# Earlier loads and new step places in the last pair of a fused attention and mixture-of-experts kernel

## The chip, the cores and the metric

One core of a Trainium2 chip. The time is the device time of one execution in microseconds (us), the median of three runs. A profile comes from one more execution, whose own time is given too.

## What is computed

```python
scores = scale * np.matmul(q, k.transpose(0, 1, 3, 2))          # B, H, S, D = 4, 8, 576, 64
scores = scores + bias.transpose(2, 0, 1)[None, :, :, :]        # a small MLP of relative positions
attn = np.exp(scores - np.max(scores, axis=-1, keepdims=True))
attn = attn / (np.sum(attn, axis=-1, keepdims=True) + 1e-09)
x = np.matmul(attn, v).transpose(0, 2, 1, 3).reshape(B * S, H * D)   # 2304 tokens of 512
logits = x @ w_gate
e_idx = np.argmax(logits, axis=1)                                # one of 8 experts for each token
for e in range(E):
    h = np.maximum(x[mask] @ w1[e], 0.0)                         # 512 to 1024
    out[mask] = gate_w[mask, None] * eom[mask, e, None] * (h @ w2[e])
```

## The kernel before, in words

**Attention.** Heads are worked on two at a time: 4 batches of 4 pairs make 16 pairs. The steps of a pair are written as words in strings, and a loop over n = 0 to 16 (L895) emits the words of one string for each n. `ORDER` serves most pairs, `LAST` is the string of n = 15 and `END` that of n = 16. A word names a step and a copying engine; each `-` at its end means one pair earlier than n, each `+` one later. `s` words score a block of 128 queries: matmuls (L763, L778), then a VectorE instruction that adds the bias and finds the maximum (L743), then the exponential on ScalarE (L748). `t` words transpose the exponentials on TensorE (L799, L811) and copy them from PSUM to `et` on ScalarE or VectorE (L803, L814). `a` words multiply with v (L831) and copy the result to `xt` (L832). PSUM has three buffers for transposes and logits (`pt`), and one for `a` (`pa`).

**v.** A pair's v lies in `vt`. The second head also needs `vb`, a copy shifted by 64 rows (loaded at L695 and L696 by the word `b`), and `vz`, a zero-padded block that GpSimd copies from `vb` (L697). There is one `vb` buffer, so the last pair's `vb` is loaded after the word `a2a-` of the pair before it.

**Work steps.** The list `work` holds generators: logits (L502), routing of a batch (L193), routing of a group of tokens (`route_group`, L245). The words `w` and `u` advance the first of them by one step. The first expert slot's loads and splits are such steps too: `first_w2` (L463) goes to the front of the list when the third score block is done, `first_w1` (L440), `first_x` (L445) and eight `first_split` (L450) go to its end.

**Experts.** The tokens are sorted into slots of 288 tokens of one expert. A slot gathers its tokens with three indirect DMAs of GpSimd (`gather`, L426), transposes them (`x`, L436 to L438), and multiplies with w1 and w2 (L1000, L1021). fp32 is split in a high and a low part. Slot 0's w1 is split in eight halves, the high part by a cast of ScalarE (L456), the low part by a subtraction on GpSimd:

```python
        nc.scalar.copy(out=w1h[c][:, h], in_=w1r[c][:, h])
        nc.gpsimd.tensor_tensor(
            out=w1l[c][:, h], in0=w1r[c][:, h], in1=w1h[c][:, h].bitcast(F32), op=ALU.subtract
        )
```

After the eighth, slot 1's w1 is loaded to the same buffers. Each later slot splits its weights with ScalarE and VectorE (L419, L420). All weights and v are loaded through the queue of SyncE (SP), which issues in program order and stops at the first load whose buffer is still in use.

**Logits.** For each third of the queries: four matmuls of `xt` (L507), a copy to `ls` on ScalarE (L530), and in the next step transposes (L537, L549) and a product with `rec` on VectorE (L540), summed into logits (L545). In the first third's first step VectorE makes `rec` from `sums`:

```python
            V.tensor_scalar(out=rec, in0=sums_t[b], scalar1=1e-9, scalar2=None, op0=ALU.add)
            V.reciprocal(out=rec, in_=rec)
```

Of the kernel before, what the change touches and what calls it, by code (L numbers as in the profile page):

```python
# [9 lines left out]
F32 = mybir.dt.float32  # L10
# [10 lines left out]
B, H, S, D = 4, 8, 576, 64  # L21
HID = 32
NPAIR = H // 2
DM, DFF, NE = 512, 1024, 8
# [4 lines left out]
G = 96  # L29
# [23 lines left out]
)  # L53

LAST = (
    "s2 s1 w u a0d- t10a- s3 u w t11a- s0 u t12a- s6 t20d- u s7 b- t04d u t01d t03a s8 u t02a a1a- "
    "s5 t00d w s4 u a2a- a0d w t14d t13a u t21d u t12a u t20d "
)

END = (  # L60
    "t10a- t11d- x a1d- x w a2a- x w x w w w w "
)


# [68 lines left out]
def attention_moe_kernel(  # L133
# [15 lines left out]
    nc = tc.nc  # L149
# [4 lines left out]
    biasp = ctx.enter_context(tc.tile_pool(name="biasp", bufs=1))  # L154
# [4 lines left out]
    vp = ctx.enter_context(tc.tile_pool(name="vp", bufs=2))  # L159
# [243 lines left out]
    w1r, w1h, w1l, w2r, xs, xg = [], [], [], [], {}, {}  # L403
# [36 lines left out]
    def first_w1():  # L440
        for i, (p, t) in enumerate(((qx, "qt0"), (qx, "qs0"), (spl, "h"), (spl, "l"))):
            w1r.append(p.tile([128, DFF], F32, name=f"w1r{i}", tag=t))
        load_w1(0)

    def first_x():  # L445
        t = nat.tile([G, 2, DM], F32, name="xg0", tag="nat")
        xg[0] = [t[:, 0, :], t[:, 1, :], vp.tile([G, DM], F32, name="xg0_2", tag="v")]
        gather(0)

    def first_split(i):  # L450
        if i == 0:
            for m, to in enumerate((w1h, w1l)):
                t = biasp.tile([128, 4, DFF], F32R, name=f"w1_{m}", tag=f"bias{m}")
                to.extend(t[:, c, :] for c in range(4))
        c, h = i // 2, slice(i % 2 * 512, i % 2 * 512 + 512)
# [4 lines that stand above are left out]
        if i == 7:  # L460
            load_w1(1)
# [11 lines left out]
    work = []  # L473
# [4 lines left out]
    def do_work(any_of=None):  # L478
        for todo in any_of or (rows, work):
            if todo:  # L480
                try:
                    next(todo[0])
                except StopIteration:
                    todo.pop(0)
                break
# [103 lines left out]
    with ExitStack() as actx:  # L589
        pool = lambda name, bufs, **kw: actx.enter_context(tc.tile_pool(name=name, bufs=bufs, **kw))  # L590
        kq = pool("kq", 2)
# [9 lines left out]
        o, n = _WHERE["psi"]  # L601
        early = hb.tile([128, 144 + 36], F32, name="early", bufs=1)
        bc, cinv = early[:, 0:144], early[:, 144:180]
        ot, n = _WHERE["tab"]
# [67 lines left out]
        kl_t, v_t, vb_t, nat_t = {}, {}, {}, {}  # L672
# [17 lines left out]

        def emit_load_vb(b, pr):

            vb = vp.tile([128, 5, D], F32, name="vb", tag="vb", bufs=1)
            src = v[b, 2 * pr + 1]
            nc.sync.dma_start(out=vb[:, 0:4, :], in_=src[0:512].rearrange("(n p) d -> p n d", p=128))  # L695
            nc.sync.dma_start(out=vb[0:64, 4, :], in_=src[512:S])  # L696
            nc.gpsimd.tensor_copy(out=vz[2][0:64], in_=vb[0:64, 4, :])  # L697
            vb_t[b, pr] = vb

        vz = []  # L700

# [132 lines left out]
        pairs = [(b, pr) for b in range(B) for pr in range(NPAIR)]  # L834
        begun = " ".join(BEGIN.values()).split()
# [31 lines left out]
        for hl in range(2):  # L867
            for i, w in enumerate((wg, wog)):
                nc.sync.dma_start(
                    out=wgb[hl * 64:hl * 64 + 64, :, hl * 16 + i * 8:hl * 16 + i * 8 + 8],  # L870
                    in_=w.rearrange("(a t d) e -> t d a e", t=2, d=64)[hl],
# [10 lines left out]
        def first(f, *a):  # L882
            yield from ()
            f(*a)

        chunks = [0, 1, 2, 3]

        def copies(c):
            return nc.scalar.copy if c == "a" else V.tensor_copy
# [5 lines left out]
        for n in range(len(pairs) + 1):  # L895
            if n == 2:
                work.extend(first(emit_zero, r0) for r0 in range((B - 1) * S, NTOK, 96))
            if n == len(pairs) - 1:
                work.append(first(first_w1))
            todo = {i: 1 for i in range(8)}  # L900
            for op in orders.get(n, ORDER).split():
                name = op.rstrip("+-")
                m = n + op.count("+") - op.count("-")
                if name == "w":
                    do_work()
                elif name == "u" and n >= len(pairs) - NPAIR:
                    do_work((work,))
                elif name == "x":
                    transpose_x(0, chunks.pop(0))
                if name in "wux" or not 0 <= m < len(pairs) or m == 0 and name in begun or m == 1 and name[0] == "p":  # L910
                    continue
                b, pr = pairs[m]
                i = int((name + "0")[1])
                if name == "s8":
                    emit_s4(b, pr)
                elif name[0] == "s":
                    emit_s(b, pr, i // 2, i % 2)
                    if m == len(pairs) - 1:

                        todo.pop(i)  # L920
                        if i < 4 and not any(j in todo for j in range(4)):
                            work.append(first(first_x))
                            work.extend(first(first_split, j) for j in range(8))
                        if i > 5 and not any(j in todo for j in (6, 7)):
                            work.insert(0, first(first_w2))
                        if i in (4, 5) and not any(j in todo for j in (4, 5)):
                            t = biasp.tile([128, 4, 4, CH], F32R, name="x", tag="bias2")
                            xs.update({j: (t[:, 2 * j], t[:, 2 * j + 1]) for j in range(2)})
                elif name[0] == "t":
                    emit_t(  # L930
                        b, pr, i, int(name[2]), copies("a" if name[0:3] in to_act and b == B - 1 else name[3])
                    )
                elif name[0] == "a":
                    emit_av(b, pr, i, copies(name[2]))
                    if i == 2 and m == len(pairs) - 2:
                        emit_load_vb(*pairs[-1])
                    if pr == NPAIR - 1:
                        work.append(emit_logits(b, i))
                        if i == 2:
                            work.append(emit_route(b))  # L940
                            if b >= B - 2:
                                work.append(route_group(b - (B - 2)))
                elif name[0] in "kp":
                    (emit_kq, emit_place)["kp".index(name[0])](b, pr, i)
                else:
                    {"l": emit_load, "v": emit_load_v, "b": emit_load_vb, "z": emit_q4}[name](b, pr)
        t = biasp.tile([G, 3, DM], F32, name="xg1", tag="bias4")
        xg[1] = [t[:, j, :] for j in range(3)]
        gather(1)
        while chunks:  # L950
            transpose_x(0, chunks.pop(0))
# [197 lines left out]
```

## Time and profile before

| | us |
|---|---|
| median of 3 runs (lowest to highest) | 645.22 (643.30 to 646.17) |
| profiled execution, its own time | 646.73 |
| its span | 644.9 |
| PE (TensorE matmul) busy | 592.7 (92%) |
| DVE (VectorE) busy | 432.6 (67%) |
| ACT (ScalarE) busy | 385.0 (60%) |
| POOL (GpSimd) busy | 83.8 (13%) |

PEld is TensorE's weight load, SP is SyncE; a name with q (SPq) is an engine's queue. The first 87 us make the bias, up to some 390 us the pairs run, then the expert slots. The page cuts the span in 40 slices of 16.1 us; the 24th, from 371 to 387 us, is the only one between the sixth and the last in which PE is busy for less than 80%.

### The profile page before, as it was taken

How to read it: one execution, taken by the hardware profiler on the slowest of the kernel's cores; microseconds unless marked ns; L12 is line 12 of the kernel's file. 1: busy time of each engine (PE TensorE's matmuls, PEld its weight loads, DVE VectorE, ACT ScalarE, POOL GpSimd, SP SyncE). 2: the span in 40 equal slices, each digit the busy share in tenths (PEclk: the TensorE clock that was granted, in tenths of full speed). 3: DMA queues.
4: the chain of work that ended last, by engine and by line, in shares of the span. 5: the costliest groups of instructions: out<-in, count | busy, mean ns of one | idle time of the engine just before them, and what ended most of it. 6: DMA issues, size and time to landing. Idle time of an engine off the chain costs nothing.

```text
span 644.9 us, 13582 instructions
## 1 busy us (share of the span) xinstructions
PE 592.7 (92%) x5036; PEld 498.2 (77%) x5036; DVE 432.6 (67%) x1011; ACT 385.0 (60%) x784; POOL 83.8 (13%) x140
## 2 busy tenths in 40 slices
PE   5887779999999999999898879999999999999992
PEld 2333368887888778887776648999999999999971
DVE  5958657766787667875898547677876465555560
ACT  5687657777776767777655644445544454454550
POOL 1000000000000000000000145021321304041010
PEclk9978979999999999999999989999999999999997
DMA  6997784765666656564643457566656555565410
GB/s 142 212 204 172 196 174 102 179 150 115 132 139 170 154 121 133 134 167 103 139 130 75 167 182 228 173 205 228 206 163 238 170 196 189 181 208 167 132 38 8
DMA packets 99846, 101.90 MB, mean 158 GB/s; under 512 B 71395, under 2 KB 71651, under 8 KB 99764
## 3 DMA queue, kind: packets, MB, share of 16 engines
q1 hardware_dynamic: 93616, 86.11, 51.9%
q0 software_dynamic: 3392, 10.03, 5.0%
q10 hardware_dynamic: 2756, 4.72, 2.1%
q8 instruction: 45, 0.74, 0.5%
q14 instruction: 37, 0.30, 0.1%
HBM read 60.73 MB, written 10.81 MB: 111 GB/s over the span
## 4 chain that ended last, share of the span: by engine, by line
PE 70%; issue 11%; DVE 6%; DMA 6%; ACT 2%; POOL 2%; SPq 1%; POOLq 0%; another core or an unknown queue 0%; DVEq 0%; ACTq 0%
PE p L1000 13%; PE p L1021 12%; PE pa L831 12%; PE ps L763 9%; PE pt L799 9%; PE pb L651 4%; PE pt L714 2%; PE ps L778 2%; DMA bias<-evl 2%; DMA vb<-in_v_dram 2%; DVE e L743 2%; PE pt L576 1%; DVE hid L640 1%; PE pt L811 1%; PE pt L1038 1%
## 5 line engine op out<-in xcount | busy, mean ns | idle before, releaser
L748 ACT ACTIVATE e<-e,nm 128x576 f32<-128x576 f32 x144 | 111.3, 774 | 56.2 <-DVE nm L743 55.1
L743 DVE CUSTOM_DVE_ANT_0 e<-ps,bias 128x576 f32<-128x576 f32 x144 | 106.1, 753 | 36.0 <-PE ps L763 29.4
L1000 PE MATMUL p<-x,w 128*128 128x288 f32 x768 | 106.8, 297 | 2.3 <-POOL w L457 1.3
L1000 PEld LDWEIGHTS p<-x,w 128*128 128x128 f32 x768 | 102.9, 188 | 4.4 <-issue 1.9
L799 PE MATMUL pt<-kept,e 128*128 128x128 f32 x576 | 82.1, 277 | 2.1 <-ACT e L748 0.9
L763 PE MATMUL ps<-qt,qs 128*128 128x288 f32 x256 | 80.2, 332 | 4.2 <-ACT evl L655 3.1
L799 PEld LDWEIGHTS pt<-kept,e 128*128 128x128 f32 x576 | 65.2, 140 | 16.7 <-issue 7.4
L831 PE MATMUL pa<-et,vt 128*64 128x256 f32 (+1 forms) x640 | 75.6, 363 | 2.2 <-ACT xt L832 1.5
L1021 PE MATMUL p<-hh,w2h 128*128 128x288 f32 x256 | 77.1, 301 | 0.0
L1021 PE MATMUL p<-hl,w2h 128*128 128x288 f32 x256 | 75.5, 295 | 0.0
L1021 PE MATMUL p<-hh,w2l 128*128 128x288 f32 x256 | 75.4, 294 | 0.0
L763 PE MATMUL ps<-kl,qs 128*128 128x288 f32 x256 | 71.6, 297 | 0.0
L651 PE MATMUL pb<-hid,w2blk 128*32 128x288 f32 x576 | 51.5, 463 | 17.9 <-DVE hid L640 8.3
L803 ACT COPY et<-pt 128x512 f32<-128x512 f32 x103 | 57.3, 578 | 14.6 <-PE pt L799 14.6
L831 PEld LDWEIGHTS pa<-et,vt 128*64 128x64 f32 x640 | 43.6, 140 | 25.4 <-issue 7.5
L1002 ACT ACTIVATE hh<-p 128x288 fp32r<-128x288 f32 x64 | 26.0, 412 | 53.5 <-PE p L1000 39.8
L763 PEld LDWEIGHTS ps<-qt,qs 128*128 128x128 f32 x256 | 48.9, 191 | 8.6 <-ACT evl L655 4.8
L651 PEld LDWEIGHTS pb<-hid,w2blk 128*32 128x32 f32 x576 | 20.6, 120 | 44.9 <-DVE hid L640 12.8
L640 DVE TENSOR_SCALAR hid<-e,early 128x576 f32<-128x576 f32 x110 | 48.8, 513 | 8.2 <-PE pb L651 5.9
L420 DVE TENSOR_TENSOR w2l<-w2r,w2h 128x1024 fp32r<-128x1024 f32 x36 | 44.0, 1224 | 12.8 <-ACT w2h L419 11.2
L420 DVE TENSOR_TENSOR w<-w1r,w 128x1024 fp32r<-128x1024 f32 x32 | 39.0, 1223 | 17.1 <-ACT w L419 17.1
L763 PEld LDWEIGHTS ps<-kl,qs 128*128 128x128 f32 x256 | 49.0, 192 | 0.0
(187 smaller groups left out, 990.9 us busy)
## 6 DMA issues: line engine op xcount, KB each, us to landing
w2r<-in_moe_w_dram SPq DMA_DIRECT2D x36, 512.0 KB
w1r<-in_moe_w_dram SPq DMA_DIRECT2D x36, 512.0 KB
kl<-qs SPq DMA_DIRECT2D x32, 288.0 KB
nat<-in_k_dram SPq DMA_DIRECT2D x16, 288.0 KB
nat<-in_q_dram SPq DMA_DIRECT2D x16, 288.0 KB
bias<-evh SPq DMA_DIRECT2D x16, 288.0 KB
bias<-evl SPq DMA_DIRECT2D x16, 288.0 KB
qs<-qt SPq DMA_DIRECT2D x16, 288.0 KB
```

The lines of the kernel that those rows point to most:

```text
L420: V.tensor_tensor(out=lo, in0=src, in1=hi.bitcast(F32), op=ALU.subtract)
L640: V.tensor_scalar(out=to, in0=src, scalar1=bc[:, r:r + 1], scalar2=0.0, op0=ALU.add, op1=ALU.max,)
L651: nc.tensor.matmul(pb[32 * t:32 * t + 32, c, 0:288], lhsT=w2f, rhs=hids[t][:, c * 288:c * 288 + 288], start=True, stop=True,)
L743: V.tensor_tensor_reduce(out=e.rearrange("p (a j) -> p a j", a=2), in0=ps[:, :, 0:n], in1=bias_ap.rearrange("p (a j) -> p a j", a=2), scal ...
L748: nc.scalar.activation(out=e, in_=e, func=ACTF.Exp, scale=-1.0, bias=nm, accum_out=sum_ap)
L763: nc.tensor.matmul(ps[:, c, 0:288], lhsT=qs[:, o:o + 128], rhs=keys[:, k0 + c * 288:k0 + c * 288 + 288], start=n == 0, stop=n == 1,)
L799: nc.tensor.transpose(pt[:, n * 256 + j * 128:n * 256 + j * 128 + 128], es[j][:, (n0 + n) * 128:(n0 + n) * 128 + 128], ident,)
L803: copy(out=et[:, n0:n0 + nn, :].rearrange("p n s -> p (n s)"), in_=pt[:, 0:nn * 256])
L831: nc.tensor.matmul(pa[p:p + 64, 0:n], lhsT=values, rhs=weights, start=i == 0, stop=i == 4)
L1000: nc.tensor.matmul(p1[:, 0:CH], lhsT=w[:, fs], rhs=x[:, c, :], start=n == 0, stop=n == 11)
L1002: nc.scalar.activation(out=hh[f], in_=p1[:, 0:CH], func=ACTF.Relu)
L1021: nc.tensor.matmul(p2[:, 0:CH], lhsT=w[f // 2][:, f % 2, ds], rhs=x[f], start=n == 0, stop=n == 23)
```

## The change

- `B` at the head of `LAST` loads the last pair's `vb` to a buffer of the pool `kq` (`vb_last`), right behind the `vb` of the pair before. `b-` goes there too. The copy of its last block to `vz` stays where it was (`emit_zb`), but is made by ScalarE.
- `W`, next in `LAST`, loads slot 0's w1; w2 follows when the third score block is done, so that SP issues w1 ahead of w2.
- `X`, behind `s5`, finishes `route_group` and emits the three gathers of slot 0. The third piece of slot 0's tokens lies in a tile with those of slot 1 now (the bias of the fifth score block was there), no more in a v buffer.
- Eight `y` between the words of `LAST` emit one `first_split` each. With these gone from `work`, each `w` and `u` from `a0d` on takes a later step of `work` than before: the last pair's logits start in `LAST` and end in `END`.
- In `END`, `a1d-` stands ahead of the first two `x`.

```diff
 LAST = (
-    "s2 s1 w u a0d- t10a- s3 u w t11a- s0 u t12a- s6 t20d- u s7 b- t04d u t01d t03a s8 u t02a a1a- "
-    "s5 t00d w s4 u a2a- a0d w t14d t13a u t21d u t12a u t20d "
+    "b- B W s2 s1 w u a0d- t10a- s3 u w t11a- s0 u t12a- s6 t20d- u s7 u t04d u t01d y t03a s8 u y "
+    "t02a a1a- y s5 X t00d w y s4 u a2a- y a0d w t14d y t13a u y t21d u y t12a u t20d "
 )
 END = (
-    "t10a- t11d- x a1d- x w a2a- x w x w w w w "
+    "t10a- t11d- a1d- x x w a2a- x w x w w w w "
 )
@@ first_x
-        xg[0] = [t[:, 0, :], t[:, 1, :], vp.tile([G, DM], F32, name="xg0_2", tag="v")]
+        t1 = biasp.tile([G, 4, DM], F32, name="xg1", tag="bias4")
+        xg[0] = [t[:, 0, :], t[:, 1, :], t1[:, 3, :]]
+        xg[1] = [t1[:, j, :] for j in range(3)]
@@ emit_load_vb
-            vb = vp.tile([128, 5, D], F32, name="vb", tag="vb", bufs=1)
+            if (b, pr) == pairs[-1]:
+                vb = kq.tile([128, 5, D], F32, name="vb_last", tag="kt")
+            else:
+                vb = vp.tile([128, 5, D], F32, name="vb", tag="vb", bufs=1)
...
-            nc.gpsimd.tensor_copy(out=vz[2][0:64], in_=vb[0:64, 4, :])
             vb_t[b, pr] = vb
+            if (b, pr) != pairs[-1]:
+                emit_zb(b, pr)
+        def emit_zb(b, pr):
+            copy = nc.scalar.copy if (b, pr) == pairs[-1] else nc.gpsimd.tensor_copy
+            copy(out=vz[2][0:64], in_=vb_t[b, pr][0:64, 4, :])
@@ the loop over n
-            if n == len(pairs) - 1:
-                work.append(first(first_w1))
...
+                elif name == "W":
+                    first_w1()
+                elif name == "B":
+                    emit_load_vb(*pairs[-1])
+                elif name == "X":
+                    while any(w.__name__ == "route_group" for w in work):
+                        do_work((work,))
+                    first_x()
+                elif name == "y":
+                    first_split(splits.pop(0))
...
-                        if i < 4 and not any(j in todo for j in range(4)):
-                            work.append(first(first_x))
-                            work.extend(first(first_split, j) for j in range(8))
...
                     if i == 2 and m == len(pairs) - 2:
-                        emit_load_vb(*pairs[-1])
+                        emit_zb(*pairs[-1])
```

ScalarE from the last score block of the last pair (L748) on, before (L803 copies to `et`, L456 casts a half of w1, L437 copies transposed tokens):

```order
L748 ACTIVATE e2_137,sums_3607<-e2_137,nm_4625 128x576
L803 COPY et_4552<-pt_4628 128x512
L748 ACTIVATE e2_137,sums_3607<-e2_137,nm_4657 128x576
L832 COPY xt1_4126<-pa_4666 128x64
L456 CAST w1_0_4694<-w1r0_4634 128x512
L803 COPY et_4698<-pt_4703 128x512
L456 CAST w1_0_4694<-w1r0_4634 128x512
L456 CAST w1_0_4694<-w1r1_4635 128x512
L803 COPY et_4698<-pt_4716 128x512
L456 CAST w1_0_4694<-w1r1_4635 128x512
L803 COPY et_4698<-pt_4730 128x512
L437 CAST x_4660<-pt_4742 128x288
```

The same place now (L759 is L748, L814 is L803, L843 is L832, L458 is L456):

```order
L759 ACTIVATE e2_137,sums_3607<-e2_137,nm_4654 128x576
L814 COPY et_4588<-pt_4662 128x512
L458 CAST w1_0_4605<-w1r1_4434 128x512
L759 ACTIVATE e2_137,sums_3607<-e2_137,nm_4675 128x576
L843 COPY xt1_4126<-pa_4679 128x64
L709 COPY vz2_894<-vb_last_4430 64x64
L458 CAST w1_0_4605<-w1r2_4435 128x512
L532 COPY ls_4714<-pt_4706 128x256
L458 CAST w1_0_4605<-w1r2_4435 128x512
L814 COPY et_4716<-pt_4723 128x512
L458 CAST w1_0_4605<-w1r3_4436 128x512 x2
L814 COPY et_4716<-pt_4756 128x512
```

Four casts now stand ahead of the copy of `xt1` (the piece shows the last of them, between the two exponentials) and four behind it, with the first copy of `ls` between the fifth and the sixth. Before, all eight stood behind it.

GpSimd before, from the `vz` copy of the pair before the last to the gather of slot 1 (L426 gathers, L457 is the subtraction):

```order
L697 COPY vz2_894<-vb_4548 64x64
L426 DMA xg0_4661<-x_dram_92,gidx0_103 96x512 x2
L426 DMA xg0_2_4662<-x_dram_92,gidx0_103 96x512
L697 COPY vz2_894<-vb_4678 64x64
L457 ISA
L457 TENSOR_TENSOR w1_1_4695<-w1r0_4634,w1_0_4694 128x512 x2
L457 TENSOR_TENSOR w1_1_4695<-w1r1_4635,w1_0_4694 128x512 x2
L457 TENSOR_TENSOR w1_1_4695<-w1r2_4636,w1_0_4694 128x512 x2
L457 TENSOR_TENSOR w1_1_4695<-w1r3_4637,w1_0_4694 128x512 x2
L426 DMA xg1_4828<-x_dram_92,gidx0_103 96x512 x3
```

and now (L459 is L457):

```order
L709 COPY vz2_894<-vb_4426 64x64
L459 ISA
L459 TENSOR_TENSOR w1_1_4606<-w1r0_4433,w1_0_4605 128x512 x2
L459 TENSOR_TENSOR w1_1_4606<-w1r1_4434,w1_0_4605 128x512
L426 DMA xg0_4657<-x_dram_92,gidx0_103 96x512 x2
L426 DMA xg1_4658<-x_dram_92,gidx0_103 96x512
L459 TENSOR_TENSOR w1_1_4606<-w1r1_4434,w1_0_4605 128x512
L459 TENSOR_TENSOR w1_1_4606<-w1r2_4435,w1_0_4605 128x512 x2
L459 TENSOR_TENSOR w1_1_4606<-w1r3_4436,w1_0_4605 128x512 x2
L426 DMA xg1_4658<-x_dram_92,gidx0_103 96x512 x3
```

The gathers stand behind three subtractions, and no `vz` copy is left between them.

VectorE before, from the copy of `xt0` after the last pair's `a0` on (L814 and L803 copy exponentials, L438 tokens):

```order
L832 COPY xt0_3902<-pa_4682 128x256
L803 COPY et_4698<-pt_4699 128x256
L814 COPY et4_891<-pt_4711 64x128
L814 COPY et4_891<-pt_4724 128x512
L803 COPY et_4698<-pt_4736 128x512
L438 TENSOR_TENSOR x_4660<-pt_4742,x_4660 128x288
L832 COPY xt0_4075<-pa_4748 128x256
L438 TENSOR_TENSOR x_4660<-pt_4760,x_4660 128x288
L438 TENSOR_TENSOR x_4660<-pt_4780,x_4660 128x288
L438 TENSOR_TENSOR x_4660<-pt_4788,x_4660 128x288
L514 TENSOR_SCALAR rec_4817<-sums_3607 128x32
L515 RECIPROCAL rec_4817<-rec_4817 128x32
```

and now (L516 is L514):

```order
L843 COPY xt0_3902<-pa_4694 128x256
L516 TENSOR_SCALAR rec_4711<-sums_3607 128x32
L517 RECIPROCAL rec_4711<-rec_4711 128x32
L814 COPY et_4716<-pt_4717 128x256
L542 TENSOR_TENSOR lt_4732<-pt_4729,rec_4711 128x256
L547 TENSOR_REDUCE logits_96<-lt_4732 128x32
L825 COPY et4_891<-pt_4737 64x128
L825 COPY et4_891<-pt_4762 128x512
L814 COPY et_4716<-pt_4774 128x512
L843 COPY xt0_4075<-pa_4780 128x256
```

The two `rec` instructions moved from behind the token copies to the place ahead of the copies of exponentials.

## Rows read from the trace of the kernel before

**Rows 1.** Windows, slot 0: length, busy of PE, PEld, DVE, ACT, POOL, PEclk, DMA.

```profile
390.19:418.14 27.95, 27.83 (x221) 27.31 (x222) 19.19 (x39) 13.60 (x27) 6.34 (x7) 1.00 0.64 199
```

**Rows 2.** Chain of waits, 368 to 392 us: start, us, what.

```profile
368.68 11.41 DMA vb<-in_v_dram
...
390.19 1.92 PE p L1000 x13
```

**Rows 3.** Timeline of PE, 369 to 406 us: start, us, instruction, [idle before <- releaser].

```profile
369.75 1.95 PE L831 MATMUL pa<-et,vt 128*64 128x256 f32 x16 [1.50 <-ACT xt L832]
...
376.81 0.47 PE L436 MATMUL pt<-kept,xg 96*128 96x96 f32 x3 [1.25 <-ACT et L803]
377.81 3.48 PE L831 MATMUL pa<-et,vt 128*64 128x256 f32 x16 [0.54 <-ACT et L803]
...
386.26 1.71 PE L1000 MATMUL p<-x,w 128*128 128x288 f32 x11
389.22 0.40 PE L1000 MATMUL p<-x,w 128*128 128x288 f32 x1 [1.25 <-POOL w L457]
...
395.01 0.38 PE L537 MATMUL pt<-kept,ls 128*128 128x128 f32 x2
...
405.29 0.32 PE L507 MATMUL pt<-xt,wgb 128*32 128x64 f32 x8
405.54 0.40 PE L519 MATMUL pt<-sums,kept 128*64 128x4 f32 x4
```

**Rows 4.** Windows of one us each, columns as in rows 1.

```profile
376.00:377.00 1.00, 0.20 (x2) 0.20 (x3) 0.28 (x1) 1.00 (x3) 0.00 (x0) 1.00 1.04 395
...
378.00:379.00 1.00, 1.00 (x6) 0.58 (x6) 0.46 (x1) 0.06 (x1) 0.00 (x0) 0.50 0.07 24
```

**Rows 5.** Timeline of ACT, 365 to 374 us.

```profile
365.86 0.37 ACT L832 COPY xt<-pa 128x256 f32<-128x256 f32 x1 [0.51 <-PE pa L831]
...
369.51 0.20 ACT L832 COPY xt<-pa 128x64 f32<-128x64 f32 x1
372.82 0.62 ACT L456 CAST w<-w1r 128x512 fp32r<-128x512 f32 x1 [3.12 <-DMA w1r<-in_moe_w_dram]
373.35 0.58 ACT L803 COPY et<-pt 128x512 f32<-128x512 f32 x1
```

**Rows 6.** Timeline of DVE, 363 to 391 us.

```profile
363.21 0.76 DVE L743 CUSTOM_DVE_ANT_0 e<-ps,bias 128x576 f32<-128x576 f32 x1 [1.31 <-PE ps L778]
...
372.18 0.42 DVE L832 COPY xt<-pa 128x256 f32<-128x256 f32 x1 [3.75 <-PE pa L831]
...
385.12 5.33 DVE L514 TENSOR_SCALAR rec<-sums 128x32 f32<-128x32 f32 x1
390.48 0.35 DVE L515 RECIPROCAL rec<-rec 128x32 f32<-128x32 f32 x1
```

**Rows 7.** The instructions of line 514, one a batch: shortest, median, longest in ns.

```profile
L514 DVE TENSOR_SCALAR rec<-sums x4: 176/177/5330, 148.3 to 385.1; 128x32 f32<-128x32 f32 x4
```

**Rows 8.** Timeline of POOL, 380 to 441 us.

```profile
380.51 9.89 POOL L457 TENSOR_TENSOR w<-w1r,w 128x512 fp32r<-128x512 f32 x8
...
439.52 0.94 POOL L426 DMA_INDIRECT xg<-x_dram,gidx  x1 [16.34 <-DMA x_dram<-x]
440.77 0.92 POOL L426 DMA_INDIRECT xg<-x_dram,gidx  x1 [0.30 <-PE pt L436]
```

**Rows 9.** The instructions of line 426, as in rows 7.

```profile
L426 POOL DMA_INDIRECT xg<-x_dram,gidx x27: 907/929/1658, 365.1 to 571.6; - x27
```

**Rows 10.** Timeline of SP's queue, 349 to 364 us.

```profile
349.79 0.52 SPq L696 DMA_DIRECT2D vb<-in_v_dram  x1
...
361.59 2.48 SPq L416 DMA_DIRECT2D w2r<-in_moe_w_dram  x4
```

**Rows 11.** Groups of DVE by form: count, busy us, mean ns, idle before and releasers.

```profile
L803 DVE COPY et<-pt 128x512 f32<-128x512 f32 x25 | 17.2, 688 | 5.7 <-PE pt L799 5.7
...
L545 DVE TENSOR_REDUCE logits<-lt 128x32 f32<-128x256 f32 x8 | 4.8, 600 | 0.3
```

More of the change, by code (lines that the diff above doesn't have):

```diff
@@ L886, in attention_moe_kernel @@
         chunks = [0, 1, 2, 3]
+        splits = list(range(8))
         def copies(c):
@@ L909, in attention_moe_kernel @@
                     transpose_x(0, chunks.pop(0))
-                if name in "wux" or not 0 <= m < len(pairs) or m == 0 and name in begun or m == 1 and name[0] == "p":
+                elif name == "W":
[8 more added lines that the diff above has]
+                    first_split(splits.pop(0))
+                if name in "wuxWBXy" or not 0 <= m < len(pairs) or m == 0 and name in begun or m == 1 and name[0] == "p":
                     continue
@@ L946, in attention_moe_kernel @@
                     {"l": emit_load, "v": emit_load_v, "b": emit_load_vb, "z": emit_q4}[name](b, pr)
-        t = biasp.tile([G, 3, DM], F32, name="xg1", tag="bias4")
-        xg[1] = [t[:, j, :] for j in range(3)]
         gather(1)
```

## The prediction

> **What bounds the kernel now.** The windows come first: in slot 0 PE is busy 27.83 of 27.95 us [rows 1], so once the expert slots run, the end moves with their start. The chain of waits shows how that start is set: it lies for 11.41 us on the load of vb, and slot 0's second matmul group begins at 390.19 [rows 2]. I call that point f1. PE's timeline then tells that vb is only one wait of several between 368 and 390. In the first of its two large v products after that, called a0, PE waited 1.50 for a ScalarE copy; then 1.25 and 0.54 for et copies; at last 1.25 for GpSimd's subtractions of w1 [rows 3]. ScalarE was late because it issues in order and stood 3.12 us in front of a cast whose w1 half had not landed [rows 5]. GpSimd was late because its vz copy waited for vb, and only then came eight subtractions of 9.89 us in all [rows 8]. A fourth loss is the clock: after a stretch with PE 0.20 busy (376 to 377) the granted clock is 0.50 (378 to 379) [rows 4], the lower level of 1.2 GHz, and the second v product, a1, took 3.48 for 16 matmuls, against 1.95 in a0 [rows 3].
>
> **What the change costs and gives, part by part.**
>
> *Loads (B, W).* Two vb loads and four of w1, with a read of the expert's number, move ahead on SP. They follow the vb of the pair before, issued at 349.79 [rows 10]. Two more vb issues (0.52 each), and four of w1 at the pace of w2's (2.48 for four) end by some 355. The w2 behind them waits for a buffer until 361.59 in any case [rows 10], so nothing is pushed back. Before, w2 and the first quarter of w1 (2.5 MB), issued from 361.59 on, let the first cast go at 372.82 [rows 5, 10], 11.2 us later; the 2 MB of w1 alone, issued from some 352 on, should be there by about 361. Casts start near 363: ScalarE no longer waits. Price 0; if a load were late, ScalarE's queue would stand, exponentials included (a rival below).
>
> *Index steps (X).* Five VectorE instructions now run ahead of the fifth block's L743, which waited 1.31 for PE [rows 6]. At some 0.2 each, like rec [rows 7], they fit there: 0.
>
> *Casts (y).* A cast holds ScalarE for 0.53 (372.82 to 373.35) [rows 5]. Four stand ahead of the copy that releases a0. Two meet waits of VectorE's results; the third stands behind the copy at 365.86, which itself had 0.51 of idle in front [rows 5]. The fourth lies between two exponentials that ran back to back: +0.52. The copy of 369.51 comes at 370.03, and a0 at 370.27 instead of 369.75. The vz copy on ScalarE (about as long as the 0.20 copy of rows 5) lies behind that copy and under a0: 0. Taken off GpSimd, it frees the subtractions from vb.
>
> *Gathers.* They stand behind three subtractions. The third of these needs the third cast (ends 366.8) and runs to 368.1; three gathers at a pitch of 1.25, the last 0.92 [rows 8], end at 371.7. Their first reader on PE is now a token transpose behind a1, near 380: 0.
>
> *Logits in LAST and END.* VectorE copied a0's result 2.43 after a0's start [rows 3, 6], so now at 372.70 to 373.12. Right behind it comes rec. **This is the dear spot.** rec takes 0.18 in three batches, but 5.33 in the last (385.12 to 390.45) [rows 6, 7], and GpSimd's row of subtractions ran from 380.51 to 390.40 [rows 8]: VectorE got on when the last of them had ended, not one of the four before. At 373.1 GpSimd is in the fourth or fifth of the subtractions, each 9.89/8 = 1.24 long: fourth from some 371.9, fifth to 374.4. The sixth needs the sixth cast, and this stands behind the copy of ls, which waits for the logits matmul of a0's copy: PE 0.2, ls 0.4, cast 0.6 after 373.12 give 374.4. I take it that GpSimd thus pauses for a moment, and that rec slips in at 374.4. The bounds are 373.1 (no wait) and 378.2 (until the eighth).
>
> The Trainium skill, page "SBUF — State Buffer", section "Who interferes with whom", speaks against this change: a VectorE tensor_scalar in its two-port mode and a GpSimd instruction exclude each other, and the second blocks until the first instruction ends. By that rule rec would wait for one subtraction, at most 1.24; the 5.33 here went past four ends, and I go by the row.
>
> *From rec to f1.* VectorE then has a reciprocal (0.35) [rows 6], a small et copy and the logits product (both like the 0.42 of rows 6), a reduction (0.60), a shorter copy and two full et copies (0.69 each) [rows 11]. PE's transposes run between these, as each needs a buffer that one of them frees. Walked in order, a1 starts at 377.8 (before: 377.81). PE is then busy enough that I take the full clock: a1 lasts 2.3, to 380.1. From a1's end (377.81 + 3.48, and 0.43 for its last four matmuls) to the first matmul of slot 0 at 386.26 it was 4.5 before [rows 3]; there are more pieces now, but none waits for a cast: 4.5 again, 384.6. The group f0 takes 1.6, its subtractions being done since 379: f1 at 386.2.
>
> *The sum.* Before, f1 stood at 390.19, with these still to come in slot 0, now done ahead of f1: two transposes at 395.01 (0.25), L507 and L519 at 405.29 (0.58) [rows 3], one transpose more (0.1). So 386.2 is to be compared with 391.1: **-4.9**. Routing steps taken earlier only trade places within slots 0 to 3: 0. Against the profiled execution's own 646.73 that is 641.8; it stood 1.5 above the median of 645.22, so the median to expect is **640.3**.
>
> **Rivals.**
>
> *VectorE is held to the end of the subtractions (slower).* If the sixth cast is ready before the fifth subtraction ends, GpSimd's row has no gap and rec waits until 378.2. It decides by tenths: gathers of 1.66 instead of 0.93, which occur [rows 9], are enough. For it: the four ends passed over. Against: the gathers beside no long VectorE work are the short ones. All later steps then stand 3.9 later, a1 at 381.7, f1 at 390.1; and PE idles five us from 374.3, more than in the stretch that brought the lower clock in [rows 4], which costs 1.8 on a1 (3.48 + 0.43 against 2.3, the difference partly made good) and up to 3 with the transposes. f1 at 392 against 391.1: **646.1**, between 644.5 and 648.5.
>
> *Each subtraction's end lets VectorE in.* A hold of one instruction: rec at 373.4, a1 at 377.1, f1 at 385.5, or -5.6: **639.6**. The 5.33 speaks against it. It is what the Trainium skill's page "SBUF — State Buffer" states in the section named above.
>
> *The clock falls all the same.* PE waits between 374.3 and 376.5 for VectorE's copies; if that brings the lower level, a1 costs 1.8 more: **642.1**. Against: before, the sparse stretch was twice as long.
>
> *The change doesn't do what it says.* w1's third and fourth quarter go to tiles from which token rows are stored; if these loads or the slower vb packets in front hold w1 beyond 363, ScalarE stands with the exponentials behind it. Two us late give 643.
>
> **How the numbers follow.** Forecast 0.42, VectorE held 0.35, clock 0.10, one instruction 0.08, late loads 0.05. The range from 638.8 to 646.8 leaves out a quarter of the held case, half of the late loads and small parts of the rest. Since two signs hold most of the chance, the likeliest case's own range is 639.2 to 641.6. Runs of this kernel tell 0.5% (3.2 us) from no change: faster means below 642.0. That takes in the forecast, the one-instruction case and half of the clock's: 0.42 + 0.08 + 0.05 = 0.55. Slower (above 648.4) is the end of the held case: 0.04. The rest, 0.41, is the same.
>
> **What the profile would show.** Right: no cast that waits for w1r; first casts near 363; a0 within 0.3 of 370.3; the eight subtractions in a group of three and one of five, done by 379; the rec instruction of the last batch 1 to 1.6 us long; a1 near 378 at full clock; f1 near 386. Wrong: rec of 4 us or more that ends with the last subtraction, PE empty from 374 to 379 and a granted clock of 0.50 behind it. The forecast also fails if a ScalarE wait for w1r stands in front of an exponential, or if the slots after f1 lose what it gained.

## The result and the profile after

The changed kernel is **slower**: 650.16 us median (645.39 to 654.76, 20 runs) against 645.67 (642.52 to 648.15, 20 runs) for the kernel before, ratio 1.0073 with the interval 1.0052 to 1.0095. The forecast of 640.3 had the wrong sign, and the range ended 3.4 us below the result.

The profiled execution took 646.54 (span 644.8), 3.6 below its own median. It cannot be set beside that of before by absolute times: its first large v product starts at 88.88, that of before at 92.48, and no line up to there is touched by the change. So I measure from an **anchor**, the first of the two large v products of the pair before the last (352.07 before, 347.60 after); ahead of it the change moves nothing but loads on SP's queue. At the anchor the changed kernel is 4.5 ahead, at slot 2 it is 1.0 behind; with 1.2 that slot 4 is shorter in this trace, the two spans come out alike, although the medians are 4.5 apart.

The windows of the kernel after, from the anchor to a0, to a1, to the first matmul of slot 0 (f0), then slots 0, 1 and 2 (each slot's end is set 0.24 behind the first matmul of the next, in every run alike). The columns are the stretch and its length; busy time and number of instructions of PE, weight loads, VectorE, ScalarE and GpSimd; the granted clock; DMA share and GB/s.

```profile
347.60:365.80 18.20, 14.87 (x139) 11.91 (x137) 10.90 (x38) 13.52 (x33) 6.25 (x8) 1.00 0.74 260
365.80:374.76 8.96, 8.56 (x53) 5.03 (x53) 3.21 (x9) 4.16 (x9) 6.40 (x7) 0.81 0.50 145
374.76:382.19 7.43, 5.88 (x75) 3.97 (x76) 3.92 (x10) 2.29 (x7) 5.53 (x6) 1.00 0.65 226
382.19:414.49 32.30, 31.82 (x235) 31.33 (x236) 20.82 (x45) 14.04 (x26) 0.91 (x1) 0.95 0.47 156
414.49:449.91 35.42, 30.95 (x228) 30.57 (x228) 25.30 (x71) 13.89 (x26) 6.54 (x6) 0.95 0.48 161
449.91:478.35 28.44, 28.44 (x229) 28.43 (x228) 19.99 (x40) 14.19 (x26) 7.99 (x6) 1.00 0.60 198
```

The same stretches of the kernel before (for slot 0 alone see [rows 1]):

```profile
352.07:369.75 17.68, 14.87 (x138) 11.91 (x136) 10.91 (x38) 11.40 (x27) 3.52 (x6) 1.00 0.39 129
369.75:377.81 8.06, 6.01 (x47) 4.05 (x47) 2.45 (x5) 3.79 (x8) 0.00 (x0) 0.98 1.02 329
377.81:386.26 8.45, 6.52 (x59) 3.88 (x60) 3.32 (x6) 3.90 (x10) 5.98 (x6) 0.81 0.19 67
386.26:418.14 31.88, 30.51 (x243) 29.20 (x243) 23.12 (x39) 14.08 (x28) 10.27 (x10) 1.00 0.64 203
418.14:448.89 30.75, 30.75 (x245) 30.72 (x244) 23.58 (x57) 14.42 (x27) 6.36 (x6) 1.00 0.67 214
```

Anchor to f0 is 34.59 after and 34.19 before, with a few steps of slot 0 already done in it. The two slots take 67.72 against 62.63: **5.1 us are lost in slots 0 and 1, where I had put zero.** PE is busy 30.95 of 35.42 in slot 1; before it was busy in all of it. Some 1.5 of the 5.1 is a fall of the granted clock in slot 0 (0.95 after, 1.00 before) that is not the change's own: e5 and e10 below have the same steps in slot 0, and it took 32.31 with such a fall in e5 and 30.79 without one in e10.

The chain of waits of the kernel after, in slot 1, shows the loss (start, length, what):

```profile
415.88 0.95 POOL out_dram L984
...
419.69 4.54 DMA out_dram<-y,sidx
...
424.35 0.69 DVE x L583
...
425.63 0.42 ACT hh L1017
...
426.08 0.47 DVE hl L1018
...
426.59 8.18 PE p L1015 x48
```

and the timelines of VectorE, ScalarE and PE around it (start, length, engine, line, operation; in brackets the idle time before it and what ended that):

```profile
412.88 0.69 DVE L583 TENSOR_TENSOR x<-pt,rec 128x512 f32<-128x512 f32 x1 [0.21 <-PE pt L578]
414.91 1.28 DVE L1056 COPY y<-pt 96x512 f32<-96x512 f32 x2 [1.33 <-DMA x_dram<-x]
419.75 0.46 DVE L1018 SCALAR_TENSOR_TENSOR hl<-p,hh 128x288 fp32r<-128x288 f32 x1 [3.56 <-ACT hh L1017]
420.68 1.23 DVE L420 TENSOR_TENSOR w2l<-w2r,w2h 128x1024 fp32r<-128x1024 f32 x1 [0.47 <-ACT w2h L419]
424.35 0.68 DVE L583 TENSOR_TENSOR x<-pt,rec 64x512 f32<-64x512 f32 x1 [2.45 <-DMA out_dram<-y,sidx]
...
418.82 0.58 ACT L1056 COPY y<-pt 96x512 f32<-96x512 f32 x1 [5.98 <-PE pt L260]
...
426.59 8.18 PE L1015 MATMUL p<-x,w 128*128 128x288 f32 x48 [4.47 <-DVE hl L1018]
```

Before, the second scatter, and the first and the last of the five products:

```profile
420.24 0.94 POOL L969 DMA_INDIRECT out_dram<-y,sidx  x1 [0.30 <-ACT hh L1002]
...
424.43 0.67 DVE L581 TENSOR_TENSOR x<-pt,rec 128x512 f32<-128x512 f32 x1
...
434.22 0.67 DVE L581 TENSOR_TENSOR x<-pt,rec 64x512 f32<-64x512 f32 x1
```

Line 583 is emit_x's product, which before came five times in slot 1 (line 581). With the routing steps advanced, four of the last batch's five token blocks fall into slot 0 and the fifth behind slot 0's output rows y. All of them take tiles of the pool x_p, which has two buffers. A block's store is issued one step later, so the fourth block still holds one buffer when slot 0's rows are written, and both rows and the fifth block pass through the other: y0, its scatter, y1 (the ScalarE copy at 418.82; its bracket names a matmul of another step, but in e4 below the same copy names the scatter), its scatter (4.54 from issue to landing), then the fifth block. The hl copies of slot 1 stand behind that block in VectorE's order: one at 419.75, the next only at 426.08. PE's next group waits 4.47 for that hl copy, which reads a PSUM buffer that it needs; its next 48 matmuls take 8.18 at a granted clock of 0.79. Before, the same five blocks stood behind both scatters and PE waited for none of them.

### The profile page after: what moved, and what is told of

It reads as the page before. It is cut to its first block, busy times and chain, and to the rows that moved or that the text cites. A ratio compares the mean times of both kernels' runs of the same rounds, so it can differ in the third digit from the quotient of the medians.

```text
span 644.8 us, 13586 instructions
## 1 busy us (share of the span) xinstructions
PE 592.1 (92%) x5036; PEld 500.5 (78%) x5036; DVE 428.5 (66%) x1011; ACT 385.9 (60%) x785; POOL 85.9 (13%) x139
## 4 chain that ended last, share of the span: by engine, by line
PE 63%; issue 16%; DVE 5%; ACT 2%; DMA 2%; POOL 1%; POOLq 0%; another core or an unknown queue 0%; ACTq 0%; DVEq 0%
PE pa L842 13%; PE p L1015 10%; PE p L1036 10%; PE pt L810 9%; PE ps L774 9%; PE ps L789 2%; PE pt L725 2%; DVE e L754 2%; PE pt L822 1%; PE pt L578 1%; PE pt L1053 1%; PE pt L436 1%; PE pb L653 1%; DMA bias<-evl 1%; PE pt L509 1%
## 5 line engine op out<-in xcount | busy, mean ns | idle before, releaser
L759 ACT ACTIVATE e<-e,nm 128x576 f32<-128x576 f32 x144 | 111.4, 774 | 54.7 <-DVE nm L754 53.1
L1015 PE MATMUL p<-x,w 128*128 128x288 f32 x768 | 108.5, 302 | 4.7 <-DVE hl L1018 4.5
L1015 PEld LDWEIGHTS p<-x,w 128*128 128x128 f32 x768 | 105.8, 193 | 5.8 <-DVE hl L1018 4.7
L653 PE MATMUL pb<-hid,w2blk 128*32 128x288 f32 x576 | 49.0, 441 | 18.2 <-DVE hid L642 8.0
L814 ACT COPY et<-pt 128x512 f32<-128x512 f32 x103 | 57.3, 577 | 13.1 <-PE pt L810 13.0
L984 POOL DMA_INDIRECT out_dram<-y,sidx x25 | 28.0, 1122 | 190.7 <-DVE y L1056 173.4
```

Of the source, the lines that this page charges most:

```text
L653: nc.tensor.matmul(pb[32 * t:32 * t + 32, c, 0:288], lhsT=w2f, rhs=hids[t][:, c * 288:c * 288 + 288], start=True, stop=True,)
L759: nc.scalar.activation(out=e, in_=e, func=ACTF.Exp, scale=-1.0, bias=nm, accum_out=sum_ap)
L814: copy(out=et[:, n0:n0 + nn, :].rearrange("p n s -> p (n s)"), in_=pt[:, 0:nn * 256])
L984: p = nc.gpsimd.indirect_dma_start(out=out, out_offset=bass.IndirectOffsetOnAxis(ap=idx, axis=0), in_=y, in_offset=None, bounds_check=NTOK ...
L1015: nc.tensor.matmul(p1[:, 0:CH], lhsT=w[:, fs], rhs=x[:, c, :], start=n == 0, stop=n == 11)
```

## Experiments

Lengths in the table are from each run's own trace, with the boundaries used above; "against before" is the difference to the median of the kernel before that was timed beside the run. All rows but e4, e2, e7 and e8 (6 or 8 executions) have 12 executions or more.

| run | median | ratio to before [95%] | against before | anchor to f0 | slots 0 and 1 |
|---|---|---|---|---|---|
| before | 645.67 | | | 34.19 | 62.63 |
| after | 650.16 | 1.0073 [1.0052, 1.0095] | +4.5 | 34.59 | 67.72 |
| e1_own_buffer | 649.0 | 1.0038 [1.0013, 1.0064] | +2.8 | 35.61 | 64.07 |
| e2_all_in_slot0 | 650.24 | 1.0067 [1.0043, 1.009] | +4.0 | 35.57 | 65.93 |
| e3_steps_late | 642.59 | 0.9946 [0.9915, 0.9976] | -3.7 | 35.58 | 60.44 |
| e4_before_steps_early | 654.94 | 1.0118 [1.0083, 1.0153] | +8.7 | 33.45 | 72.36 |
| e5_two_buffers | 645.42 | 0.999 [0.9967, 1.0013] | -0.5 | 33.80 | 61.35 |
| e6_loads_alone | 642.97 | 0.9961 [0.9943, 0.9978] | -2.9 | 31.76 | 62.17 |
| e7_late_cast | 640.82 | 0.9937 [0.9919, 0.9954] | -5.1 | 33.43 | 58.91 |
| e8_short_end | 640.89 | 0.993 [0.9907, 0.9952] | -5.0 | 32.29 | 59.52 |
| e9_steps_late_again | 644.17 | 0.9957 [0.9934, 0.998] | -2.7 | 33.96 | 58.91 |
| e12_late_cast_again | 641.7 | 0.9937 [0.9906, 0.9969] | -5.1 | 33.89 | 58.91 |
| e10_buffers_and_cast | 643.25 | 0.9954 [0.993, 0.9979] | -3.6 | 33.86 | 59.83 |
| e11_pause_for_rec | 644.47 | 0.9963 [0.9938, 0.9988] | -2.4 | 33.67 | 60.64 |

### Is it the steps, and is it the buffers? (e3, e4, e1, e2, e5)

**e3_steps_late**, on the changed kernel:

```diff
 SLOT_WORK
-    "f0 f3 d0 d1 d2 d2 d3",
-    "f0 f0 f1 f3 f3 f4 f6 f7 f7 d0 d1 d2 d2 d3",
+    "f3 d0 d2",
+    "f1 f3 f3 f4 f6 f7 f7 d0 d1 d2 d2 d3",
```

> The changed kernel with its loads, casts, gathers and the order of the last pair, but the routing steps of slots 0 and 1 put back: three steps in slot 0 instead of seven and twelve in slot 1 instead of fourteen, so that the five token blocks come between the groups of slot 1 as in the kernel before, behind slot 0's scatters. Theory (the buffer): only the gain ahead of the slots is left, which the two traces put at 2.8 us up to slot 0's second group, and slot 4's wait of 1.2 that is gone: 641.5 to 643.5. Rival (the front): if the change loses ahead of the slots, the time is at or above the kernel before, 646 or more.

Measured: 642.59, as the theory had it; with the repeat below, 2.7 to 3.7 us below the kernel before. Slots 0 and 1 took 60.44, 7.3 us less than in the changed kernel; both traces have a fall of the clock in slot 0. One part of the expectation fell: slot 4's 1.2 did not come, so that saving in the changed kernel's trace was of that execution, not of the change.

**e4_before_steps_early**, on the kernel before:

```diff
 SLOT_WORK
-    "f0 f3 d0 d1 d2 d2 d3",
+    "f0 f1 f2 f3 f4 f5 f6 f7 d0 d1 d2 d2 d3",
```

> The kernel before, its last pair untouched, with six steps more in slot 0 (thirteen instead of seven), so that four token blocks of the last batch lie in slot 0 and the fifth in slot 1 behind slot 0's output rows, as in the changed kernel. Theory (the buffer): PE waits 4 to 5 us in slot 1 for the product of the fifth block and the clock falls behind it: 5 to 7 us slower than the kernel before, 650 to 653. Rival (the loads or the front): without the changed loads there is no loss, 645 to 647.

Measured: 654.94, 8.7 us slower without any of the change's loads, casts or gathers, and more than the 5 to 7 expected. In slot 1 (35.11) PE waited 4.29 for the hl copy. Slot 0 grew too, from 31.88 to 37.25, with a fall of the clock (0.95) and 2.83 of PE idle against 1.37; how much of that the moved steps cost no run tells apart. The chain of waits in slot 1 has the same links, and ScalarE's copy of y1 names the first scatter:

```profile
425.50 0.58 ACT L1041 COPY y<-pt 96x512 f32<-96x512 f32 x1 [5.81 <-DMA out_dram<-y,sidx]
...
426.36 4.39 DMA out_dram<-y,sidx
...
430.87 0.69 DVE x L581
...
432.60 0.47 DVE hl L1003
...
433.11 7.92 PE p L1000 x46
```

The two runs show that the loss comes from the routing steps' place. How it comes about took three more.

**e1_own_buffer**, on the changed kernel, in emit_x:

```diff
+            if b == B - 1 and qb == 4:
+                p, tag = vp, "v"
             x = p.tile([128, H, D], F32, name="x", tag=tag)
```

> The changed kernel, with one buffer more: the fifth token block of the last batch gets a tile of its own (in the pool of the v tiles, where one is free) instead of one of the two that it shares with slot 0's output rows. Theory (the buffer): its product no longer stands behind the two scatters of slot 0, so PE's 4.47 us in slot 1 go, and with them the 1.8 us by which the 48 matmuls behind them were longer; some 6 us faster than the changed kernel, 643 to 645, about 1 us below the kernel before; slot 1 near 30 us instead of 35.9. Rival (ScalarE's queue): the ScalarE copy of slot 0's second output part still waits for the first scatter, with all of slot 1's ReLUs behind it; if that is what stops PE, slot 1 stays above 34 and the time near 650. Rival (the front): the loss is the half clock at a0 and its 2.02 us; then nothing changes, 650.

Measured: 649.0, far less back than I expected; slot 1 was 31.77, not 30. The fifth block no longer waited, but the chain of waits (first line) and ScalarE's timeline show the other user of the buffer, the second output part:

```profile
421.63 2.79 DMA out_dram<-y,sidx
...
424.57 0.58 ACT L1058 COPY y<-pt 96x512 f32<-96x512 f32 x1 [5.91 <-PE pt L260]
424.70 0.33 ACTq L587 DMA_DIRECT2D x_dram<-x  x1
425.05 0.41 ACT L1019 ACTIVATE hh<-p 128x288 fp32r<-128x288 f32 x1
```

It starts 2.0 after GpSimd's scatter of the first part had been issued (421.63 and 0.95 long), whose buffer it takes, and 0.15 after that scatter had landed; the PE matmul in the bracket belongs to another step. All ReLUs of slot 1 stand behind it, and PE still waited 1.93. The rival on ScalarE's queue was half right.

**e2_all_in_slot0**, on the changed kernel:

```diff
 SLOT_WORK
-    "f0 f3 d0 d1 d2 d2 d3",
-    "f0 f0 f1 f3 f3 f4 f6 f7 f7 d0 d1 d2 d2 d3",
+    "f0 f1 f3 f4 f5 f6 d0 d1 d2",
+    "f1 f3 f6 f7 f7 d0 d1 d2 d2 d3",
```

> The changed kernel with the steps of slots 0 and 1 placed otherwise: nine steps in slot 0 instead of seven, so that all five token blocks and the last store come ahead of slot 0's output rows; slot 1 has ten. Theory (the buffer): the output rows then wait only for stores issued some microseconds earlier, PE waits under 1 us at the start of slot 1, and the time is that of the run with a buffer of its own, 642 to 645. Rival (number of steps): if it is the token steps in slot 0 as such that cost (VectorE and ScalarE fuller there), slot 0 gets longer than 31 us and the time stays at 648 or above.

Measured: 650.24. Slot 1 was clean at 28.59, but slot 0 took 37.34. That length is what the rival named, yet PE was busy for only 33.98 of it, at a granted clock of 0.91: a wait and falls of the clock, not full engines. ScalarE's timeline:

```profile
406.25 0.40 ACT L1042 COPY ytqt<-p 128x288 f32<-128x288 f32 x1 [2.44 <-PE p L1036]
413.87 0.33 ACTq L585 DMA_DIRECT2D x_dram<-x  x1
414.29 1.05 ACT L419 CAST w<-w1r 128x1024 fp32r<-128x1024 f32 x1 [7.64 <-DMA xg<-x_dram,gidx]
```

The stores of the token blocks write x_dram, and the gathers for slot 2 read it. Now two stores come ahead of these gathers in program order and three behind, and the third has to wait for them at the head of ScalarE's queue, 7.64 us in all. PE then waited 3.09 for VectorE's part of a token transpose.

**e5_two_buffers**, on the changed kernel (the fifth block as in e1):

```diff
@@ first_w2
-        t = biasp.tile([128, 4, 2, DM], F32, name="w2r", tag="bias3")
-        w2r.extend(t[:, i] for i in range(4))
+        t = biasp.tile([128, 9, DM], F32, name="w2r", tag="bias3")
+        w2r.extend(t[:, 2 * i:2 * i + 2] for i in range(4))
+        spare[3] = t[:, 8]
...
@@ emit_x
+            if qb in spare and b == B - 1:
+                x = spare[qb].rearrange("p (h d) -> p h d", h=H)
...
```

> The changed kernel with all its steps where the change put them, but two buffers more for the last batch's token blocks: the fourth lies in the unused end of the tile of w2r, the fifth in the pool of the v tiles. So no output row of slot 0 shares a buffer with a block whose store comes after it, and neither the fifth block's product nor ScalarE's copy of the second output part waits for a scatter. Theory (the buffers are the whole loss of slots 0 and 1): PE waits no more in slot 1, the two slots together take 61 to 62.5 us (changed kernel 67.7, steps put back 60.4, fifth block alone in another buffer 64.1), and the time is 642 to 645. Rival (the number of steps in slot 0 costs too): the slots stay above 63.5, the time above 646.

Measured: slots 0 and 1 at 61.35, as expected, with no PE wait in slot 1. The windows of the two slots:

```profile
384.68:416.99 32.31, 31.83 (x235) 31.34 (x236) 21.02 (x46) 14.04 (x26) 0.92 (x1) 0.95 0.50 155
416.99:446.03 29.04, 29.04 (x228) 29.01 (x228) 24.94 (x71) 14.23 (x26) 7.10 (x6) 1.00 0.65 196
```

So in the traces two more buffers take away 6.4 of the 7.3 us; 0.9 stay with the steps in slot 0, and stay in e10 too (59.83 against 58.91). The time, 645.42, is just above the expected 642 to 645. Against before it is -0.5, where the changed kernel has +4.5 and the steps put back -2.7 and -3.7: in the medians the buffers give back 5.0 of 7.2 to 8.2, less than in the traces. The fall of the clock in slot 0 (0.95 above) costs some 1.5 in this trace, but e3's has it too; what the rest is stays open.

### What the loads are worth (e6)

The kernel before, with the change's emit_load_vb and emit_zb and its words B and W, and in LAST:

```diff
-    "s2 s1 w ...
+    "b- B W s2 s1 w ...
-... u s7 b- t04d ...
+... u s7 t04d ...
```

> The kernel before with the loads of the change alone: vb of the last pair and w1 issued at the start of the last pair, its vz copy on ScalarE; casts, gathers and routing steps stay steps of the work list (one step fewer, since w1's load has left it). Theory (the casts and GpSimd wait only for these loads): no cast waits for w1 and the subtractions no longer for vb, so a0 stands at 1.50 after its copy as before, f1 comes 3 to 5 us sooner than before, the slots stay as they were but for one step, 641 to 644. Rival (VectorE is held): the reciprocal's input still meets GpSimd's eight subtractions in one row and nothing is won, 645 to 647.

Measured: 642.97, -2.9: the theory. The loads alone give what all of the change gives with its steps put back (-2.7 and -3.7). f0 comes 31.76 after the anchor, against 34.19 before. One part was missed: a cast ran in front of the copy of xt1 here too, and PE waited 2.02 ahead of a0, not 1.50. VectorE was not held for long either: rec took 0.68. It ended 0.04 behind a subtraction, at 379.29, although the next had begun at 379.25; in a window between these two the fifth busy figure, GpSimd's, shows two instructions:

```profile
378.65 0.68 DVE L514 TENSOR_SCALAR rec<-sums 128x32 f32<-128x32 f32 x1
...
379.26:379.28 0.02, 0.02 (x2) 0.02 (x1) 0.02 (x1) 0.00 (x0) 0.02 (x2) 1.00 0.00 0
```

### The casts and VectorE's reciprocal input (e7, e8, e11, e10)

**e7_late_cast**, on e3:

```diff
-... y s5 X t00d w y s4 u a2a- y a0d w t14d ...
+... y s5 X t00d w s4 u a2a- y a0d y w t14d ...
```

> The run with the steps put back, and the fourth cast moved from between the two exponentials to behind the first large v product a0. Theory: the cast's 0.52 us goes from in front of a0, PE's wait there is 1.5 instead of 2.03, and the time is 0.3 to 0.6 below that run, within what the rounds tell: 641.5 to 643. If the granted clock falls because of this wait, it falls less often, and the spread of 639.5 to 647.5 of that run narrows to its lower half. Rival: the clock falls for another reason (about 361, ahead of it); then the spread stays.

Measured: 640.82, better than expected. PE's wait in front of a0 fell from 2.03 to 1.51. But a1 came no sooner (25.42 after the anchor; 25.49 in e5), because two subtractions now run in a row when VectorE comes to rec. VectorE, GpSimd, and then windows of 0.02 us of this run, in which the fifth busy figure is GpSimd's:

```profile
369.81 1.80 DVE L516 TENSOR_SCALAR rec<-sums 128x32 f32<-128x32 f32 x1
```

```profile
369.06 6.26 POOL L459 TENSOR_TENSOR w<-w1r,w 128x512 fp32r<-128x512 f32 x5
```

```profile
370.30:370.32 0.02, 0.02 (x2) 0.00 (x0) 0.02 (x1) 0.00 (x0) 0.02 (x2) 1.00 0.00 0
...
371.56:371.58 0.02, 0.02 (x1) 0.00 (x0) 0.02 (x1) 0.02 (x1) 0.01 (x2) 1.00 1.13 205
```

At 370.3 the next subtraction had begun before the last one ended, and rec was passed over. At 371.57 GpSimd stood for 0.01 us, its next cast only just done, and rec ended 0.04 later. The 5.33 of before [rows 6, 8] looks alike: at each of the four ends that rec passed over, the next subtraction had begun 0.03 earlier. But so it had in e6, where rec got in. A pause of GpSimd let VectorE in wherever one came; what decides at an end without a pause stays open.

**e8_short_end**, on e7:

```diff
 END
-    "t10a- t11d- a1d- x x w a2a- x w x w w w w "
+    "t10a- t11d- a1d- x x w a2a- x x w w "
 SLOT_WORK
-    "f3 d0 d2",
+    "f0 f0 f0 f3 d0 d2",
```

> The run with the late cast, and three routing steps fewer between the last pair and slot 0 (now steps of slot 0's first group), the token transposes ahead of the second logits step. Theory: from the start of the second large v product a1 to slot 0's first matmul it takes 6.5 us instead of 8.5 (two waits of 1.0 to 1.3 for ScalarE's copies leave PE's path), 1.5 to 2 us below the run with the late cast: 639.5 to 641.5. Rival (slot 0 pays): the steps stand in front of slot 0's ReLUs on VectorE and ScalarE, and slot 0 is longer by as much: 642 to 643.

Measured: 640.89, in the upper half of the theory, and the same as e7. a1 to f0 went from 8.01 to 6.87, and slot 0 from 28.16 to 28.77: the rival took half of it.

**e11_pause_for_rec**, on e8 (casts five to eight one place later):

```diff
-... a2a- y a0d y w t14d y t13a u y t21d u y t12a u t20d "
+... a2a- y a0d w y t14d t13a u y t21d u y t12a u y t20d "
```

> The run with the short end, and the fifth cast moved behind the ls copy, so that GpSimd has only the fourth subtraction to do when VectorE comes to rec and then stands without work. In the run with the late cast rec took 1.80: it passed over the end of the fourth subtraction, where GpSimd's next one began before the last had ended, and got in at the end of the fifth, where GpSimd waited 0.01 us for a cast. Theory (VectorE gets in at a pause of GpSimd): rec ends with the fourth subtraction, 0.5 to 0.7 long, a1 starts about 1 us sooner (24.2 to 24.7 after the second product of the pair before instead of 25.42), and the time is 0.5 to 1.2 below the short end's: 639.5 to 640.5. Rival (something else binds a1: ScalarE's et copies behind the casts): a1 where it was and 640.5 to 641.5.

Measured: rec took 0.18. It began 0.13 before the fourth subtraction ended, and no other followed, so that VectorE did not wait; but a1 stood at 25.64 and the time was 644.47, -2.4 against before where e8 has -5.0. The wait moved on: behind rec, VectorE waited 0.59 for PE's transposes, and PE 0.33 and 0.35 for copies. f0 was 8.03 behind a1, 1.16 more than in e8, and in slot 0 PE waited 1.35 for an hl copy.

**e10_buffers_and_cast** is e5 with the cast of e7:

> The changed kernel, its routing steps where the change put them, with the two buffers more and the fourth cast behind a0. Theory: with the buffers slots 0 and 1 lose nothing but 0.9 us against the steps put back (61.35 against 60.44 in the traces), and with the late cast the clock stays up: 641 to 643, against 645.4 for the two buffers alone. Rival (the cast is worth only its 0.52 us): 644.5 to 645.5.

Measured: 643.25, just above the theory's range and below the rival's.

### Repeats (e9, e12)

> The run with the steps put back once more, unchanged, beside the run with the late cast. Open: its times lay in two heaps, 639.5 to 641.8 and 643.4 to 647.5, and its profile, from the upper heap, shows a fall of the granted clock at 361, before any cast that the late cast moves. If the fourth cast's place decides over the clock (PE's empty stretch in front of a0 is 0.5 us longer with it), the heaps are there again and the median is 642 to 644, 1 to 3 us above the late cast's. If the falls were chance or this chip's, both kernels come out alike, within 0.6 us.

> The run with the late cast once more, unchanged. If the cast's place decides over the clock: 640.3 to 641.3, all runs below 643, no granted clock below 1.00 between the last pair's start and slot 1. If the falls are chance: some runs above 643, as in the run with the steps put back.

Measured: 644.17 and 641.7. The late cast is 2.5 below here; in the first pair it is 1.4 below, and in e10 against e5 3.1, each taken against the kernel before beside it. All three point one way, but the intervals of each pair overlap, and this time e12 has runs up to 647. Not settled: the cast itself is worth 0.5 in the traces, and whether its place also decides over the clock no run shows. What the repeat does show is the price of the clock, on the same code. The windows of e3, and of e9, up to a0 and of slot 0:

```profile
352.21:372.01 19.80, 16.46 (x139) 13.50 (x137) 10.89 (x38) 13.56 (x33) 6.42 (x8) 0.91 0.72 248
...
387.79:417.48 29.69, 29.69 (x219) 29.68 (x220) 18.57 (x42) 14.04 (x27) 1.19 (x2) 0.94 0.47 145
```

```profile
351.17:369.34 18.17, 14.84 (x138) 11.88 (x137) 10.90 (x38) 13.53 (x33) 6.51 (x8) 1.00 0.79 269
...
385.13:413.29 28.16, 28.16 (x219) 28.15 (x220) 18.51 (x42) 13.94 (x27) 1.19 (x2) 1.00 0.50 153
```

Two falls cost 1.6 and 1.5 us, and one execution has them while the other has not.

The best versions are e7, which stood at 0.9937 twice, and e8 (0.993), which these runs do not tell apart: 5 us below the kernel before and some 9 below the changed one.

## Why the prediction was wrong, point by point

- **The step that failed: "Routing steps taken earlier only trade places within slots 0 to 3: 0".** It was worth +7.3 (67.72 against 60.44 with the steps put back; in the medians 1.0073 against 0.9946 and 0.9957). In its place the runs showed a wait: slot 0's output rows and the fifth token block pass through one buffer, and PE stands 4.47 in slot 1. I had followed the queues of the moved steps but not the pool that they allocate from, nor x_dram, which they write and the gathers read. It was also the condition that I named last ("if the slots after f1 lose what it gained").
- Loads, price 0: right. The first cast ran at 358.37, 10.8 after the anchor, behind an et copy and not behind w1.
- Casts, +0.52 in front of a0: right to the hundredth: 18.20 after the anchor against 17.68. In e7 it went, and rec's wait ate it.
- rec slips in when GpSimd pauses: right for this kernel. By my absolute times rec was to come 21.03 after the anchor and get in at 22.33; e9 has 20.94 and 22.22, rec 1.28 long. In the changed kernel's own trace rec took 0.17, because a0 was late and GpSimd stood already.
- a1 25.73 after the anchor: 25.46 in e9 and 25.49 in e5. In the profiled execution 27.16, since a0, after PE had stood for 2.02, ran at the lower clock level (1.2 GHz): 3.62 for 16 matmuls instead of 1.95.

```profile
365.80 3.62 PE L842 MATMUL pa<-et,vt 128*64 128x256 f32 x16 [2.02 <-ACT xt L843]
370.24 0.17 DVE L516 TENSOR_SCALAR rec<-sums 128x32 f32<-128x32 f32 x1
374.76 1.95 PE L842 MATMUL pa<-et,vt 128*64 128x256 f32 x16
```

- a1 to f0 in 6.8: mis-sized. It was 7.43 here and 8.3 to 8.5 in e3, e5 and e9; in those three ScalarE stood idle 1.1 to 1.9 in front of its ls copy (0.23 in the changed kernel's trace) behind the logits matmuls; no row gives the cause, which stays open.
- Rivals. VectorE held to the end of the subtractions: no run with the earlier loads showed it (rec took 1.80 at most). One instruction at a time: e7 speaks against it, as VectorE was passed over at one end and got in at the next; e6, where it got in at the first end, looks like it. The Trainium skill, page "SBUF — State Buffer", section "Who interferes with whom", says that the second engine blocks for the whole instruction of the first. These rows agree that it blocks, and show that the end of one instruction does not always let it in. The clock fell all the same: a fall came in the profiled execution, but at a0 and at f0, and not at a1, where the rival had it.
- The -4.9 for what is ahead of the slots: with the steps put back, the two runs gave -3.7 and -2.7. Mechanism right, size one to two us too large, most of it in a1 to f0. That e7 comes to -5.1 is no confirmation, since it has another order of casts.

## What to carry to other kernels

When a step moves across another allocation of the same pool, replay the pool as well as the queues: who gets which buffer, when its last reader is issued, and what stands behind the waiting instruction on its engine. Do the same for memory that one step writes and others read: a store that moves behind a gather waits for it (7.64 in e2). If work is to run earlier, give it its own buffers first, and time the loads alone: here they gave as much (-2.9) as the whole change with its steps put back.

## What the runs showed that I had not expected

- VectorE gets past a row of GpSimd instructions through a gap of 0.01 us (e7). At an end where the next instruction has already begun it was passed over in e7 (370.3) and four times in the kernel before, yet got in once (379.29 in e6).
- Of two executions of the same code, one had two falls of the granted clock and lost 3.15 us between the anchor and slot 2 (e3 96.02, e9 92.87). Half a per cent in one trace can thus be the clock alone.
- The code ahead of the first pair took between 88.88 and 92.84 in these traces, so stretches have to be compared from an anchor near the change.
